# A fused linear-attention and MLP kernel: a division moved ahead of features, two transposes and a product regrouped, a new order table

## The chip, the cores and the metric

The kernel runs on one core of a Trainium2 chip. The core has five engines that run side by side: TensorE (PE, matrix products and transposes into PSUM), VectorE (DVE), ScalarE (ACT), GpSimd (POOL, used here to issue transfers and to make constants) and SyncE (SP, which issues transfers). The metric is the device time of one execution in microseconds (us); lower is better.

## The reference

Cosformer attention over 8 batches, 8 heads, 576 positions, 64 dimensions, then an MLP with a squared ReLU:

```python
q_p, k_p = phi(q, cos_w, sin_w), phi(k, cos_w, sin_w)   # relu(x)*cos(pos), relu(x)*sin(pos): 128 features
kv  = einsum('bhsf,bhsd->bhfd', k_p, v)
z   = sum(k_p, axis=2)
num = einsum('bhsf,bhfd->bhsd', q_p, kv)
den = einsum('bhsf,bhf->bhs', q_p, z)[..., None] + 1e-06
x   = (num / den), laid out as (4608, 512)
h   = x @ w_in                                           # (4608, 2048)
out = relu(h)**2 @ w_out                                 # (4608, 512)
```

## The kernel before

**Tiling.** A batch's 576 positions are four query blocks j = 0..3 of 128 and a tail of 64; the tails of all batches form a ninth token set, "batch 8". For each batch the attention part does: load k, q, v; features (`cos b.j`, `sin b.j`, each for k and q at once, on ACT or DVE; `.t` is the tail); `kv b` (40 small products into one PSUM tile, with z in a column of ones) and its copy `kvz b`; q's features transposed (`qT`, by TensorE and a copy `qTc` for batches 0 and 1, by a transposing DMA `qTd` on SP for later ones); `num b.j` (8 products); `div b.j` on DVE (den + eps, reciprocal, multiply) into x; x transposed (`xT`/`xTc`, or `xTd` by DMA). `vs b.i` spreads v into a tile that all batches share.

**The MLP.** Token blocks are 256 wide (tok 0 = queries 0 and 1, tok 1 = queries 2 and 3). Batch 0, batch 1 and half of batch 2 use plain products: `H b.s.tok half` is 8 matmuls of 128x256 for two blocks of hidden units, followed by a relu `r` (ACT or DVE) and, for pairs, a square `q`. `Y0.a0..15` and `Y0.b0..15` are batch 0's output products, one hidden block each. The other products use a scheme of seven half-size products in place of eight (Strassen's, in Winograd's form): `G b.s.P1..P7` for the first matrix and `Y b.P1..P7` for the second, with sums `xs`, `w1s`, `w2t`, `S` on DVE and copies between PSUM tiles (`seed`, `u2`, `s5`) and results (`c11`, `c12`, `c21`, `c22`) on ACT and DVE. Stores are `Y b.st0/1`.

**What sets the order.** Each engine runs its instructions in program order. The first part (`begin`, L1312) is written by hand: constants, loads, batch 0's k features, the features of queries 0 and 1, kv in two halves, their numerators and divisions. `warm` puts in matmuls on zeros so that TensorE is not idle; their results are not used. After that comes the table `ORDER`: a list of operation names in the order of emission, a `*` meaning ACT where ACT or DVE would do. `Plan.run` (L220) walks the table, picks tile slots with a small model of due times (`plan.given` tells it when things of the first part are ready) and `o.emit` then puts each operation out. The times in the model decide slots only; on the chip each operation waits for its data.

**PSUM.** Tiles of the MLP come from the pool `x` with 6 one-bank slots; `n` (numerators and kv) has one slot of two banks.

**Transfers.** POOL issues, in this order: k's tails of batch 0, q of queries 0 and 1, v, q of queries 2 and 3, w1 in four quarters (`w1.0`–`w1.3`; cast to bf16 on the way), q's tails, w2's first quarter, and then `loads_of_1` (L1433): q and its tails, k and its tails, w2's second quarter, v, w2's third and fourth quarter, all for batch 1 but for w2. After that come batch 2's loads as the table places them (`ldv2.0`, `ldq2`, `ldk2`, ...). The tile of q and k, `kq`, has one slot, so q1 waits until batch 0's features have read it. Half `vs` tiles of batch 1 lie in the slots of `y`; from batch 2 on they share one slot of their own. `Y0.x4` is the first product that reads w2's second quarter, `Y0.x8` the third, `Y0.x12` the fourth; `w2t1` needs all four. SP issues the later batches' loads, the transposing DMAs and most stores.

**The pair of output products.** `plan_pair` (L1122) has two shapes. With `apart` (batch 8 only, before) the first product's two token halves go into two one-bank tiles, each half of the second product is added and copied out alone at the very end, and the stores are cut into halves. Without it both halves share a tile. In both, `P1` is one operation of 16 matmuls, and one or two `seed` copies follow it.

Of the kernel before, what the change touches and what calls it, by code (L numbers as in the profile page):

```python
# [11 lines left out]
F32 = mybir.dt.float32  # L12
# [10 lines left out]
ORDER = """  # L23
qT0.2 xT0.k2 xT0.k3 qTc0.2 qT0.3 xTc0.k3* H0.0.00.0 xTc0.k2 qTc0.3* num0.2 H0.0.00.1 div0.2
H0.0.00.2 H0.1.00.0 H0.1.00.1 H0.1.00.2 H0.0.00r num0.3 H0.1.00r* xT0.2 H0.3.00.0 div0.3 xTc0.2*
H0.2.00.0 H0.3.00r xT0.3 H0.1.01.0 xTc0.3* H0.0.11.0 H0.1.10.0 H0.0.11r* H0.1.00q* H0.1.11.0
f0.t1 H0.1.10r H0.2.11.0 H0.1.11r* w1s1 f0.t0* H0.0.10.0 H0.2.00r* H0.1.01r* H0.2.11r H0.0.01.0
H0.0.10r* H0.1.11q* qT0.4 H0.1.10q Y0.a0 Y0.a1 H0.0.01r* Y0.b0 qTc0.4* Y0.a2 H0.3.11.0 Y0.a3
H0.3.11r Y0.b1 H0.3.00q Y0.b2 H0.3.11q* H0.2.10.0 w1s2 H0.3.01.0 H0.2.10r* sin1.3 H0.3.10.0
H0.3.01r* cos1.t Y0.b3 sin1.t H0.3.10r* H0.2.01.0 cos1.0 H0.3.10q* sin1.0 qT1.4 Y0.a4 H0.2.01r*  # L30
cos1.2 ldv2.0 Y0.b4 qTc1.4* sin1.1 Y0.b5 sin1.2* Y0.b6 cos1.3 Y0.a5 cos1.1* vs1.0 Y0.a6 Y0.a7
vs1.1 Y0.b7 ldq2 vs1.2* qT1.3 qT1.0 qTc1.3 ldk2 kv1 qTc1.0 ldkt2.0 H0.1.01q qT1.1 ldkt2.1 kvz1*
qT1.2 qTc1.1* ldv2.2 Y0.b8 Y0.b9 qTc1.2* num1.1 Y0.b10 div1.1 ldqt2.1 Y0.a8 H0.3.01q* Y0.a9
ldqt2.0 w1s4 Y0.a10 xT1.1 num1.2 Y0.b11 div1.2 Y0.b12 ldkt3.1 Y0.b13 ldkt3.0 w2t1 Y0.b14 vs2.0*
num1.0 ldqt3.0 xT1.2 Y0.a11 div1.0 xTc1.1* ldqt3.1 ldv2.1 Y0.b15 xTc1.2* Y0.a12 w2t2 Y0.c11*
Y0.a13 xT1.0 num1.3 xTc1.0* Y0.a14 div1.3 Y0.a15 Y0.c10* H1.1.01.0 Y0.c00* Y0.st1 w2t3 Y0.c01*
xT1.3 H1.2.00.0 xTc1.3* Y0.st0 H1.1.01r H1.2.01.0 sin2.0* sin2.1 H1.2.10.0 cos2.2 cos2.0*
H1.1.10.0 cos2.1 H1.2.10r sin2.3* H1.3.00.0 qTd2.0 cos2.3 H1.3.10.0 H1.3.00r* sin2.2 cos2.t*
H1.2.01r H1.0.01.0 vs2.1* H1.3.10r qTd2.1 H1.1.11.0 vs2.2 sin2.t* H1.2.00r H1.0.00.0 H1.0.01r*
w2t4 kv2 ldv3.2 H1.0.00r* H1.1.11r* H1.3.00q H1.0.10.0 H1.1.01q kvz2* ldv3.0 ldk3 num2.1  # L40
H1.0.10r* H1.1.00.0 div2.1 ldq3 H1.1.10r* H1.0.11.0 ldqt4.1 H1.1.00r* H1.3.10q H1.2.11.0
H1.1.10q H1.0.11r* H1.1.00q* H1.1.11q num2.2 H1.3.11.0 div2.2 H1.2.11r* H1.3.01.0 H1.3.11r*
ldkt4.1 vs3.2 H1.3.11q num2.3 ldv4.2 H1.3.01r* Y1.P1 div2.3 H1.3.01q* Y1.S1 xTd2.1 num2.0
Y1.seed vs3.0* Y1.S2 Y1.P2 div2.0 ldv3.1 Y1.P6 Y1.c11 xTd2.0 Y1.S3 num1.4 Y1.u2* sin3.1 Y1.P5
cos3.0* qTd2.2 sin3.0 cos3.1 sin3.3* Y1.P7 sin3.2 qTd3.0 Y1.s5* cos3.2 cos3.3* Y1.S4 H2.1.10.0
qTd3.1 vs3.1 H2.0.11.0 sin3.t* div1.4 H2.1.10r* H2.0.00.0 cos3.t* ldv4.0 H2.1.00.0 H2.0.00r ldk4
# [36 lines left out]
div5.4 cos7.0* G5.2.P6 G5.2.P2 sin7.0 Y4.P7 G5.1.c21q* xTd5.2 Y4.c12 vs7.1* G5.2.u2 Y4.st0
G5.3.P1 G5.2.c11r G5.2.P7 G5.3.seed cos7.1 G5.2.P3 sin7.t* G5.3.P5 Y4.c22 qTd7.0 G5.3.P2 cos7.3
G5.3.s5* G5.3.P6 G5.3.c11r* G5.2.c22r Y4.P4 G5.3.c11q* G5.1.c12q sin7.3 G5.3.u2* G5.2.P4 cos7.2
Y4.c21* G6.0.P1 cos7.t* G5.3.P7 qTd7.1 G5.3.P3 G5.2.c21r* G5.3.c22r kv7 G6.0.seed G5.2.c12r
G5.3.c22q* G5.3.c12r qTd7.2 G6.0.P2 G5.3.P4 G5.3.c12q G6.0.c11r* Y5.P1 G5.3.c21r* xs6.1 xs6.2
kvz7* Y5.S1 G5.3.c21q* G6.0.P5 num7.0 Y5.seed xs6.3 G6.0.P6 Y5.S2 G6.1.P1 G6.0.u2* Y5.P2
G6.0.s5* div7.0 G6.1.seed Y5.S3 num7.1 G6.1.P2 G6.1.P6 div7.1 G6.0.P3 G6.1.u2* G6.0.P7 Y5.S4
G6.1.c11r* xTd7.0 G6.1.P7 Y5.c11* num7.2 G6.1.P5 xs6.4 Y5.P5 Y4.st1 div7.2 G6.1.s5* G6.0.c22r  # L90
G6.1.c22r num7.3 Y5.s5* G6.1.P3 G6.1.c22q Y5.P6 G6.1.c11q* G6.1.c12r G6.2.P1 Y5.u2 G6.0.P4
div7.3 G6.1.P4 Y5.P7 G6.1.c21r* G6.0.c12r xTd7.1 G6.2.seed G6.1.c12q G6.0.c21r* G6.2.P5 Y5.c22
G6.1.c21q* G6.3.P1 G6.2.P6 G6.2.s5* Y5.P3 G6.2.u2* Y5.P4 Y5.c12 G6.3.seed G6.3.P6 Y5.c21*
G6.2.P2 G6.3.u2 Y5.st1 G6.3.P5 G6.2.c11r* G6.2.P3 G6.3.s5 G6.2.P7 G6.3.P2 G6.2.c22r G6.3.P3
G6.3.c11r* G6.3.P7 G6.3.c12r G6.3.c11q* G7.0.P1 G6.3.c22r num7.4 G7.0.seed G6.2.P4 G6.3.c22q
G6.3.P4 G6.2.c21r Y6.P1 G6.3.c21r* xs7.1 xs7.2 G6.2.c12r G7.0.P5 G6.3.c21q Y6.seed G7.1.P1 xs7.3
G7.0.P6 G6.3.c12q G7.0.P2 G7.0.s5 Y6.P2 G7.0.c11r* Y6.S1 G7.1.seed G7.0.P3 Y6.S2 Y6.c11* G7.1.P6
# [184 lines left out]
def kernel(  # L282
# [836 lines left out]

    def plan_pair(b, apart=False):  # L1122

# [424 lines left out]
```

## Time and profile before

| what | value |
|---|---|
| median of 3 runs | 274.11 us (273.96 to 275.32) |
| profiled execution, its time | 273.9 us |
| its span, first to last instruction | 271.8 us |
| TensorE busy | 263.3 us, 97% of the span |
| DVE, ACT, POOL busy | 226.7 (83%), 187.6 (69%), 28.9 (11%) |
| granted TensorE clock, mean | 0.998 |
| moved by DMA | 53.00 MB |

Times in the text are microseconds from the start of the span. A busy share is that of the whole span; the warming matmuls on zeros count as busy. A wait of TensorE is told with what released it. "To landing" is the time from a transfer's issue until its data is there. The "DMA share" of a stretch is the mean busy share of the 16 transfer engines, and can come out a little above 1 when packets overlap.

### The profile page before, as it was taken

The page shows a single profiled execution, that of the slowest core. Times are in us where ns is not written, and L with a number is a line of the kernel's source. Part 1 is how long each engine was busy: PE and PEld are TensorE (multiplying, and loading weights), DVE is VectorE, ACT ScalarE, POOL GpSimd, SP SyncE. Part 2 cuts the span into 40 slices and gives each one's busy share as a digit, 9 for nine tenths or more (in the row PEclk, how much of TensorE's full clock was granted, in tenths as well). Part 3 has the DMA queues.
Part 4 walks back from the last instruction along what each step waited for, and adds up shares of the span by engine and source line. Part 5 has one row for each costly group of instructions (what it writes and reads, how often), then busy time and mean ns, then how long its engine had stood idle before and what let it go on. Part 6 is the DMA issues. An engine that isn't in the chain of part 4 may idle for free.

```text
span 271.8 us, 6753 instructions
## 1 busy us (share of the span) xinstructions
PE 263.3 (97%) x2787; PEld 224.4 (83%) x2792; DVE 226.7 (83%) x403; ACT 187.6 (69%) x292; POOL 28.9 (11%) x47
## 2 busy tenths in 40 slices
PE   8799999999999999999999999999999999999994
PEld 3568767699778888989888998899888888888883
DVE  3874696998997999799989899989849978789952
ACT  5665695888567997889689968996554534955600
POOL 8924446200000000000000000000000000000000
PEclk9999999999999999999999999999999999999999
DMA  7999999897999999999997999680321021010215
GB/s 219 316 204 268 317 280 306 294 299 204 296 218 268 287 272 265 380 148 225 288 286 184 208 325 300 171 159 11 110 56 61 10 112 57 38 42 0 80 43 191
DMA packets 79006, 53.00 MB, mean 195 GB/s; under 512 B 52064, under 2 KB 74592, under 8 KB 78976
## 3 DMA queue, kind: packets, MB, share of 16 engines
q1 hardware_dynamic: 71344, 38.28, 55.0%
q0 software_dynamic: 7040, 13.76, 19.1%
q10 hardware_dynamic: 592, 0.52, 0.6%
q8 instruction: 22, 0.36, 0.5%
q14 instruction: 8, 0.07, 0.1%
HBM read 36.70 MB, written 9.44 MB: 170 GB/s over the span
## 4 chain that ended last, share of the span: by engine, by line
PE 84%; DMA 6%; DVE 4%; POOL 3%; issue 1%; ACT 0%; SPq 0%; POOLq 0%; ACTq 0%
PE ya L461 17%; PE yb L461 14%; PE hb L461 13%; PE hps L461 10%; PE hc L461 8%; PE ha L461 8%; PE yh L461 5%; DMA w1sb<-in_moe_w_in_dram 5%; PE kz L461 3%; PE num L461 3%; PE yc L461 1%; DVE gs L458 1%; DMA qpTt<-fet 1%; PE tq L622 1%; DVE fe L450 1%
## 5 line engine op out<-in xcount | busy, mean ns | idle before, releaser
L461 PEld LDWEIGHTS <-w1sb 128*128 128x128 bf16 x736 | 70.5, 98 | 10.8 <-issue 1.5
L461 PEld LDWEIGHTS <-gs 128*128 128x128 bf16 x512 | 49.7, 98 | 5.8
L461 PEld LDWEIGHTS <-gT 128*128 128x128 bf16 x448 | 43.1, 98 | 10.3 <-issue 0.5
L442 ACT ACTIVATE gT<-gT 128x1024 bf16<-128x1024 bf16 x38 | 39.6, 1060 | 4.0 <-DVE gT L455 2.0
L461 PE MATMUL hps<-xT,w1sb 128*128 128x256 bf16 x320 | 37.9, 273 | 1.2 <-ACT gT L436 0.8
L450 DVE TENSOR_SCALAR fe<-kq,cols 128x1024 bf16<-128x1024 f32 (+1 forms) x44 | 30.1, 722 | 5.2 <-DMA kq<-in_k_dram 3.5
L461 PEld LDWEIGHTS <-w1s 128*128 128x128 bf16 x312 | 29.8, 98 | 3.3
L461 PE MATMUL ya<-w2sb,gT 128*128 128x256 bf16 x256 | 30.6, 273 | 0.4 <-ACT yb L432 0.4
L461 PE MATMUL hb<-xs,w1sb 128*128 128x256 bf16 x208 | 30.1, 272 | 0.0
L448 ACT ACTIVATE fe<-kq,cols 128x1024 bf16<-128x1024 f32 (+1 forms) x28 | 27.6, 1027 | 2.9 <-DMA kq<-in_k_dram 1.6
L461 PE MATMUL ha<-xT,w1sb 128*128 128x256 bf16 x176 | 26.4, 273 | 0.0
L444 DVE TENSOR_TENSOR gT<-gT 128x1024 bf16<-128x1024 bf16 x34 | 23.0, 687 | 1.6 <-ACT gT L436 1.3
L604 DVE TENSOR_TENSOR xp<-num,den 128x512 bf16<-128x512 f32 (+1 forms) x33 | 22.2, 675 | 1.1
L455 DVE CUSTOM_DVE_ANT_0 gT<-hb,s 128x512 bf16<-128x512 f32 x26 | 17.8, 687 | 3.8 <-PE hb L461 3.7
L436 ACT ACTIVATE gT<-ha 128x512 bf16<-128x512 f32 x23 | 13.8, 600 | 9.5 <-PE ha L461 9.3
L436 ACT ACTIVATE gT<-hps 128x512 bf16<-128x512 f32 x27 | 15.6, 595 | 6.4 <-PE hps L461 6.4
L432 ACT COPY hb<-ha 128x512 f32<-128x512 f32 x26 | 15.2, 586 | 6.4 <-DVE gT L438 3.1
L458 DVE TENSOR_TENSOR gs<-gT 128x2048 bf16<-128x2048 bf16 x16 | 19.5, 1217 | 0.1
L455 DVE CUSTOM_DVE_ANT_0 gT<-hc,u 128x512 bf16<-128x512 f32 x26 | 17.5, 685 | 1.1 <-PE hc L461 0.9
L436 ACT ACTIVATE gT<-hb 128x512 bf16<-128x512 f32 x20 | 11.9, 601 | 6.7 <-PE hb L461 6.6
L461 PE MATMUL hc<-xs,w1s 128*128 128x256 bf16 x104 | 15.6, 272 | 0.0
L461 PE MATMUL hb<-xs,w1s 128*128 128x256 bf16 x104 | 15.6, 272 | 0.0
(111 smaller groups left out, 415.0 us busy)
## 6 DMA issues: line engine op xcount, KB each, us to landing
out_dram<-y SPq DMA_DIRECT2D x16, 512.0 KB, 3.6
vs<-in_v_dram SPq DMA_DIRECT2D x10, 512.0 KB, 4.6
kq<-in_k_dram SPq DMA_DIRECT2D x5, 1024.0 KB, 8.2
kq<-in_q_dram SPq DMA_DIRECT2D x5, 1024.0 KB, 9.9
w1sb<-in_moe_w_in_dram POOLq DMA_DIRECT2D x4, 512.0 KB, 12.0
w2sb<-in_moe_w_out_dram POOLq DMA_DIRECT2D x4, 512.0 KB, 10.7
kq<-in_q_dram POOLq DMA_DIRECT2D x2, 1024.0 KB, 11.5
kq<-in_k_dram POOLq DMA_DIRECT2D x2, 1024.0 KB, 11.7
```

Of the source, the lines that this page charges most:

```text
L432: (nc.scalar.copy if e == "ACT" else nc.vector.tensor_copy)(out=out, in_=in_)
L436: nc.scalar.activation(out=out, in_=in_, func=ACTF.Relu)
L442: nc.scalar.activation(out=out, in_=in_, func=ACTF.Square)
L444: nc.vector.tensor_tensor(out=out, in0=in_, in1=in_, op=ALU.mult)
L448: nc.scalar.activation(out=out, in_=in_, func=ACTF.Relu, scale=col)
L450: nc.vector.tensor_scalar(out=out, in0=in_, scalar1=0.0, scalar2=col, op0=ALU.max, op1=ALU.mult)
L455: nc.vector._custom_dve(dve_ops.TENSOR_ADD_SAT, out=out, in0=in0, in1=in1, s0=BIG, s1=0.0)
L458: nc.vector.tensor_tensor(out=out, in0=in0, in1=in1, op=op)
L461: nc.tensor.matmul(out=out, lhsT=lhsT, rhs=rhs, start=start, stop=stop, skip_group_check=True)
L604: nc.vector.tensor_tensor(out=x, in0=n4[:, :, :, 0:D].rearrange("p b (k l) d -> p b k l d", l=2), in1=r.rearrange("p b (k l) -> p b k l", l=2)
L622: nc.tensor.transpose(t[:, h, :], src, ident[:, :])
```

## The change

The table is new throughout. Its beginning, as it was:

```diff
-qT0.2 xT0.k2 xT0.k3 qTc0.2 qT0.3 xTc0.k3* H0.0.00.0 xTc0.k2 qTc0.3* num0.2 H0.0.00.1 div0.2
-H0.0.00.2 H0.1.00.0 H0.1.00.1 H0.1.00.2 H0.0.00r num0.3 H0.1.00r* xT0.2 H0.3.00.0 div0.3 xTc0.2*
-H0.2.00.0 H0.3.00r xT0.3 H0.1.01.0 xTc0.3* H0.0.11.0 H0.1.10.0 H0.0.11r* H0.1.00q* H0.1.11.0
-f0.t1 H0.1.10r H0.2.11.0 H0.1.11r* w1s1 f0.t0* H0.0.10.0 H0.2.00r* H0.1.01r* H0.2.11r H0.0.01.0
...
-cos1.2 ldv2.0 Y0.b4 qTc1.4* sin1.1 Y0.b5 sin1.2* Y0.b6 cos1.3 Y0.a5 cos1.1* vs1.0 Y0.a6 Y0.a7
```

and as it is:

```diff
+xT0.k0 sin0.2* cos0.3 xTc0.k0 xT0.k2 ldv2.0 cos0.2* qT0.2 sin0.3* qTc0.2 xT0.k3 xTc0.k2 qT0.3
+xTc0.k3* H0.1.00.0 num0.2 H0.1.00.1 H0.1.00.2 H0.0.00.0 H0.0.00.1 H0.0.00.2 div0.2 qTc0.3*
+num0.3 div0.3 xT0.2 H0.3.00.0 xT0.3 H0.2.00.0 xTc0.2 xTc0.3* H0.1.10.0 H0.1.10r H0.2.10.0
+H0.2.00r* H0.0.01.0 H0.0.01r* H0.1.01.0 H0.1.01r* H0.0.10.0 H0.2.10r* H0.1.11.0 f0.t1 H0.0.00r
+H0.1.00r H0.1.00q H0.3.00r Y0.a0 f0.t0* qT0.4 H0.0.10r H0.1.10q H0.0.11.0 H0.0.11r* w1s1 Y0.a1
+Y0.a2 H0.2.11.0 qTc0.4* H0.2.11r* w1s2 w1s4 Y0.a3 H0.2.01.0 cos1.3 H0.1.11r* H0.2.01r* H0.3.10.0
+H0.3.10r* H0.3.10q sin1.0* Y0.b0 Y0.b1 Y0.b2 Y0.b3 H0.3.01.0 H0.3.00q sin1.3* sin1.t cos1.t
+H0.3.11.0 H0.3.11r cos1.1 Y0.b4 H0.3.01r* Y0.b5 Y0.b6 Y0.a4 Y0.a5 cos1.2* sin1.1* qT1.4 qTc1.4*
+vs1.1* sin1.2 qT1.3 ldqt2.1 Y0.a6 Y0.a7 cos1.0 qT1.0 vs1.0 qTc1.3* vs1.2 kv1 H0.3.11q* qT1.1
+H0.1.01q Y0.a8 Y0.a9 Y0.b7 qTc1.1 kvz1* num1.1 ldq2 qTc1.0 qT1.2 H0.1.11q* Y0.b8 Y0.b9 Y0.b10
+div1.1 xT1.1 qTc1.2* num1.2 ldk2 H0.3.01q* ldkt2.1 w2t1 Y0.b11 Y0.b12 Y0.b13 Y0.b14 div1.2 xT1.2
+w2t2 xTc1.1* num1.0 ldqt2.0 div1.0 Y0.b15 xTc1.2* Y0.c10* w2t3 Y0.a10 vs2.0* Y0.a11 Y0.a12
...
+num2.3 H1.1.11q H1.3.11r* H1.3.01.0 H1.3.01r* H1.3.01q* Y1.P10 div2.3 num2.0 Y1.seed Y1.P11
+Y1.seed1 ldqt4.1 H1.3.11q vs3.2 Y1.P20 vs3.0* Y1.P21 Y1.c111* Y1.S1 Y1.S2 Y1.P6 xTd2.1 div2.0
+Y1.S3 Y1.c110 Y1.u2* cos3.0* sin3.1 cos3.1 cos3.2* sin3.0 sin3.2 sin3.3* num1.4 div1.4 cos3.3*
+Y1.P5 ldv4.2 Y1.S4 ldv3.1 vs3.1 H2.1.10.0 xTd2.0 xs2.1 H2.1.10r* qTd2.2 H2.0.11.0 H2.0.11r*
```

The rest of the code. In `plan_pair`, batch 1's pair is made with `apart` too (but with whole stores; `last` now marks batch 8's), and with `apart` the first product is two operations, P10 and P11, each with its own seed:

```diff
-    def plan_pair(b, apart=False):
+    def plan_pair(b, apart=False, last=False):
...
-        ys = [buf(p, [P, 2, DM], F32, "y") for p in (("vs", "y") if apart else ("y", "y"))]
+        ys = [buf(p, [P, 2, DM], F32, "y") for p in (("vs", "y") if last else ("y", "y"))]
...
-                        start = first and hb == 0 and (t == 0 or len(spaces) > 1)
+                        start = first and hb == 0 and (t == t0 or len(spaces) > 1)
...
-            after = [w[1]] + (seeds if apart else [e11])
+            after = [w[1]] + ([p1] if apart else [e11])
...
-        after = [w[0], sum5.get(b), begun.get(0)]
-        p1 = prod(1, A, block(0, 0), lambda: w2_block(0, 0), True, after, accs)
+        p1, seeds = None, []
+        for t in range(len(accs)):
+            t1 = t + 2 // len(accs)
+            after = [w[0], sum5.get(b), begun.get(0)] if p1 is None else [p1]
+            p1 = prod(1, A, block(0, 0), lambda: w2_block(0, 0), True, after, accs[t : t + 1], t, t1)
+            seeds.append(
+                ev(
+                    f"seed{t or ''}",
+                    {"ACT": act((t1 - t) * n)},
+                    lambda e, t=t, t1=t1: copy(e, run[:, t:t1, :], bank(accs[t])),
+                    [p1],
+                    [accs[t], run],
+                )
+            )
...
-            p = prod(2, A, lhs, lambda: w2_block(1, 0), False, seeds, accs[t : t + 1], t, t + 1)
+            after = seeds[t : t + 1]
+            p = prod(2, A, lhs, lambda: w2_block(1, 0), False, after, accs[t : t + 1], t, t + 1)
...
-                plan_pair(b - 1)
-        plan_pair(B, True)
+                plan_pair(b - 1, b == 2)
+        plan_pair(B, True, True)
```

In the part written by hand, one of qpT's copies goes from DVE to ACT; the features of queries 2 and 3, the turns (transposes) of x's first two blocks and their copy, and the call of `loads_of_1` go out of it, so that the division of the second head group follows the first directly:

```diff
-            copy("DVE", qpT[0, 0][:, j, 0:HH], tqs[j][0][:, :, :])
+            copy("ACT" if j else "DVE", qpT[0, 0][:, j, 0:HH], tqs[j][0][:, :, :])
...
         div_mul(na[:, :], dens[0][:, 1], x_of(0, 2))
-        cos_part("DVE", 0, 2, q_)
-        sin_part("ACT", 0, 2, q_)
         warm(2, "x0")
         nb = numerators(1)
         div_den(nb[:, :], dens[1])
-        tx = spare("x1", [P, 2, 2, P], BF16, "tx")
-        for kb in range(2):
-            turn_x(tx[:, kb], kb)
-        dst = xT[0, 0][:, 0:2, :].rearrange("p k (j c) -> p k j c", j=2)
-        copy("ACT", dst, tx[:, :, :, :])
         for i in range(2):
             part = nb[:, :, 2 * i * E1 : 2 * (i + 1) * E1]
             div_mul(part, dens[1][:, 1, :, 2 * i : 2 * (i + 1)], x_of(2 + i, 3 + i))
-        cos_part("DVE", 0, 3, q_)
-        sin_part("ACT", 0, 3, q_)
         warm(4, "x0")
-        loads_of_1()
```

They become table operations (`xT0.k0`, `xTc0.k0`, `cos0.2`, `sin0.2`, `cos0.3`, `sin0.3`), and `loads_of_1` is called in the table's loop when the last of the four features has been put out:

```diff
+    def plan_query(j, after):
+        made = []
+        for name, part in (("cos", cos_part), ("sin", sin_part)):
+            made.append(
+                plan.op(
+                    f"{name}0.{j}",
+                    both(0.62, 0.41),
+                    lambda e, part=part: part(e, 0, j, q_),
+                    [after],
+                    [fe[0, 1]],
+                )
+            )
+        return made
...
+        fq0 = {(1, j): plan_query(j, q0) for j in (2, 3)}
+        first = fq0[1, 2] + fq0[1, 3]
...
             o.emit(o.engine)
+            if o in first:
+                first.remove(o)
+                if not first:
+                    loads_of_1()
```

The due times given to the table's model are changed by some tenths too.

241 lines of the change are left out of this document (120 added, 121 removed).

## The prediction

> **What bounds the kernel now.** I read the page's head first, then TensorE's busy time in stages that I cut at its own landmarks, then its waits.
>
> ```profile
> span 271.8 us, 6753 instructions
> PE 263.3 (97%) x2787; PEld 224.4 (83%) x2792; DVE 226.7 (83%) x403; ACT 187.6 (69%) x292; POOL 28.9 (11%) x47
> ```
>
> ```profile
> 14.00:17.45 3.45, 3.17 (x38) 2.08 (x36) 2.52 (x8) 2.40 (x5) 0.06 (x1) 1.00 1.23 205
> 17.45:22.51 5.06, 4.76 (x59) 4.00 (x57) 3.56 (x9) 2.45 (x4) 2.08 (x3) 1.00 1.25 211
> 22.51:36.90 14.39, 14.34 (x119) 11.42 (x121) 8.73 (x13) 9.78 (x16) 8.20 (x11) 1.00 1.12 317
> 36.90:51.91 15.01, 14.85 (x164) 9.17 (x165) 12.39 (x24) 11.09 (x17) 6.23 (x9) 1.00 1.10 292
> ...
> 70.00:83.00 13.00, 11.69 (x122) 9.91 (x120) 12.67 (x21) 7.54 (x10) 0.00 (x0) 1.00 1.13 243
> 83.00:268.10 185.10, 185.04 (x1989) 165.57 (x1986) 160.81 (x277) 130.70 (x206) 0.00 (x0) 1.00 0.63 163
> ```
>
> Columns: stage, its length, then busy time of PE, its weight loads, DVE, ACT, POOL, then granted clock, DMA share, GB/s. From 22.51 us on, TensorE (PE) is the bound. It idles 0.05 in 22.51–36.90, 0.16 in 36.90–51.91, 1.31 in 70–83 and 0.06 in the 185 us after that. So the change, which keeps every product, can win at most about 1.6 us here, plus what the start gives. The DMA share is above 1 from 14 us to 52 us: the transfer engines have no free time there.
>
> ```profile
> PE hps L461 <- ACT gT L436: 0.8, 1, 0.8
> ...
> PE ya L461 <- ACT yb L432: 0.4, 1, 0.4
> PE hps L461 <- DMA w1sb<-in_moe_w_in_dram: 0.3, 1, 0.3
> ```
>
> These are the waits the change could touch: the wait for w1's third quarter (to 22.51), the one of Y1.P2 for its seed (to 70.61) and the one of a batch 2 product for a PSUM buffer (to 81.98). The last has a chain behind it: ACT evicts only after `sin3.t`, which waited 2.17 us for qTd2.2 to free its tile.
>
> Next, the transfers on POOL's queue: when each was issued (timeline), and how long until it landed (DMA issues, cut to one issue each).
>
> ```profile
> 17.39 0.90 POOL L502 DMA_DIRECT2D kq<-in_q_dram  x1 [4.13 <-ACT xT L432]
> 26.52 0.76 POOL L418 DMA_DIRECT2D w2sb<-in_moe_w_out_dram  x1
> 28.19 0.75 POOL L512 DMA_DIRECT2D vs<-in_v_dram  x1 [0.92 <-DMA w2sb<-in_moe_w_out_dram]
> 35.95 0.80 POOL L512 DMA_DIRECT2D vs<-in_v_dram  x1
> ```
>
> ```profile
> w2sb<-in_moe_w_out_dram POOLq DMA_DIRECT2D x1, 512.0 KB, 10.3
> ...
> vs<-in_v_dram POOLq DMA_DIRECT2D x1, 512.0 KB, 9.9
> ...
> w2sb<-in_moe_w_out_dram POOLq DMA_DIRECT2D x1, 512.0 KB, 11.1
> ```
>
> The same sum for each issue gives the landings, in queue order: w2's first quarter 27.9, q1 30.8, k1 33.9, w2's second quarter 26.52 + 10.3 = 36.8, v1's halves 28.19 + 9.9 = 38.1 and 39.4, w2's third 42.8, its fourth 35.07 + 11.1 = 46.2, v2's first half (35.95, 11.6) 47.55. They come one after another without a gap, so each costs those behind it its own time: a 512 KB half of v 1.3 us (36.8 to 38.1 to 39.4).
>
> ```profile
> 36.68 0.39 PE L622 MATMUL tq<-ident,fet 128*128 128x128 bf16 x4
> 36.90 3.62 PE L461 MATMUL yh<-w2sb,gT 128*128 128x512 bf16 x15
> ```
>
> The first product that reads w2's second quarter (Y0.a4) starts at 36.90, a tenth after it landed, and nothing before it waits. TensorE and the queue are level there.
>
> **The change, part by part.**
>
> *POOL's queue.* The new table has ldv2.0 (512 KB for batch 2) ahead of cos0.2 and sin0.3. But batch 1's loads are now issued inside the table loop, once the last of the four features of queries 2 and 3 has been issued. So ldv2.0 goes to POOL before q1, k1, w2's later quarters and v1, where it went last before. It waits for no data: the vs tile has no earlier user. Everything from q1 to w2's fourth quarter lands 1.3 us later: k1 35.2, w2's second quarter 38.1, v1's last piece 41.1, w2's third 44.1, its fourth 47.5. Behind that the queue is as long as before, so q2 and k2 are not later.
>
> Bounds for that price: 0 if the queue had room, 1.4 by v2's own turn (46.2 to 47.55). I take 1.3, because the share above 1 leaves no room. The Trainium skill ("DMA: Bandwidth & Descriptors", queues, rings and completion order) says that each engine consumes a ring's descriptors in ring order, and the trace agrees, as landings follow issues. The same page (anatomy of one DMA) puts the moving part at bytes/436e3 us, for 512 KB an estimate of 1.2 us; with it the term below would be 0.1 smaller.
>
> Now TensorE. Ahead of w2's second quarter the new table has 16 H products (0.873 each by the 8-matmul rows), eight Y0 steps (0.437), two numerators (0.24) and three transposes (0.22): 18.6 us. From 17.45 that ends at 36.05. I find four small waits on the way: the second division's buffer (0.15), div0.3 before xT0.3, which now has one product ahead of it and not two (0.3), Y0.a0 (0.55) because f0.t1 holds DVE until q0's tail lands (25.54 in the trace) and four DVE steps of 0.68 follow, and a PSUM buffer (0.1). So it is ready at 37.15 and goes on at 38.15. Before, the same point (without qT1.4, which moves behind it) was 36.68. **+1.47.**
>
> After it: kv1 needs the last DVE features and vs1.2. Nine DVE steps from k1 at 35.2 (four features of 0.73, two tails of 0.5, two squares of 0.69, one relu of 0.68) and two spreads (0.69, 0.6) end at 42.5; TensorE is there at 42.3. With a wait's usual lag **+0.25** (0 to 0.6). w2t1 needs all of w2, so DVE stands at it until 47.5 and div1.2 and div1.0 come 1.2 (w2t) + 1.1 each behind; xT1.2 and xT1.0 wait 0.2 and 0.1 by my count, and one more division could. **+0.4** (0 to 1.0).
>
> *The division ahead of the features, qpT's copy on ACT.* ACT sat idle 0.55 at 11.24–11.79, so the copy (0.59) is free there, and DVE's v spread and the second kv sums come 0.45 earlier. den1 starts at about 14.35 and not 15.26, xp is done at 15.5 and not 16.45. But q's second half lands at 7.12 + 7.7 = 14.8, three features on ACT at 0.67 each end at 16.9, and qT0.3 starts at 16.95 (16.99 before); w1's first quarter lands at 17.4 too. So the first H product stays at 17.45. x's turns move 0.22 of transposes and one 0.47 copy into the table, beside the features. **0** here, and w2's second quarter covers it: TensorE has 1.0 to spare before 38.15. Without that cover its cost is the +0.47 that 37.15 stands behind 36.68.
>
> *Y1's first product in halves.* Two half seeds (0.37 by the last `y<-ya` 128x256 copy) in place of one of 0.57, and the second product goes at once, with nothing between; the 0.36 seed wait goes. But P6 comes next and needs S2. From num2.1 DVE has three divisions (1.1), three squares (0.69), one relu, vs3.2 (0.6) and two sums (1.22): 9.1 us; TensorE has 8.5 to do until P6. P6 then waits 0.6 where before it came right after P2. **0** (−0.36 to +0.3). The two extra PSUM banks that Y1 now holds come back with c110 and c111 before batch 2's products.
>
> *The wait at 82 us.* In the new table H2.1.10's and H2.0.11's evictions stand ahead of sin3.t on ACT, so the 2.17 us that ACT stands there no longer hold a PSUM buffer. **−0.98** (the idle of 80–90 in 10 us steps; −1.3 to 0).
>
> After 83 us the same products run, dense before, and the tail of 3.7 us (c111 0.42, two stores) is the same steps. Sum: 1.47 + 0.25 + 0.4 + 0 − 0.98 = **+1.1**: span 272.9. The profiled run took 273.9 for 271.8, and the median is 274.11, 0.2 above it, so 274.11 + 1.1 = **275.2 us**.
>
> **The rivals.**
>
> *DVE keeps the delay (slower).* If the later w2 and k1 push DVE's whole list (12.67 of 13.00 busy in 70–83), the wait at 82 us stays: S4, xTd2.0 and qTd2.2 all hang on it. For it: in 60–83 the chain before already runs through DVE's xp, gT, gs and fe. Against: w1s4 (1.22) moves from 45.7 to about 32 us, which DVE has free. It decides from where DVE, not TensorE, starts S1. Price: 1.47 + 0.25 + 0.4 + 0 = 2.1 with no gain, 276.2; with the upper ends (0.6, 1.0) 3.1, 277.2.
>
> *The transfer is hidden.* If queue order does not pass the 1.3 on, w2's second quarter lands at 36.8 and TensorE's own 37.15 decides: +0.47, no late kv1 or w2t1, −0.98 later: −0.5, 273.6. With the small early waits absent as well (36.85, +0.17) and the seed's 0.36 won, −1.2, 272.9. Against it is the DMA share.
>
> *The change doesn't do what it says.* The start gives nothing, as worked out, since w1 and q land when they did; that is in the forecast already and in both rivals.
>
> **How the numbers follow.** Forecast 0.45 (its own range 274.4 to 276.0), DVE rival 0.33 (276.0 to 277.2), hidden transfer 0.22 (272.7 to 274.1). The range 273.3 to 276.9 leaves out about the lowest third of the hidden case and the top of the DVE case, near 2 in 10. A measurement of this kernel can tell about 0.5% (1.37 us) from no change: 272.74 to 275.48. Faster takes a quarter of the hidden case and a little of landing jitter: 0.07. Slower takes a third of the forecast (0.15) and nearly all of the DVE rival (0.31): 0.46. The rest, 0.47, is the same.
>
> **What would show it.** Right: POOL issues a vs half before q1; w2's second quarter lands at about 38.1; a TensorE wait for DMA w2sb near 37–38 us of 0.5 to 1.3; Y0 done at 54 (51.9 before); no ACT gT wait near 82. Wrong: Y0.b4 before 37.5, or a vs issue behind w2's last quarter; a TensorE wait over 0.6 between 70 and 83 speaks for the DVE rival. A span below 271.5 would say that the queue had room and that my account of its order is wrong.

## The result, and the profile after

The changed kernel took 276.0 us (median of 20 runs, 274.25 to 276.95) beside 273.69 us for the kernel before (20 runs, 272.67 to 276.13): a ratio of 1.0069, 95% interval 1.0046 to 1.0091. That is some 1.9 us, 1.3 to 2.5: a small slowdown, but clear of the noise. Measured again on another chip, it was 1.0055 (1.0023 to 1.0087). The forecast was 275.2 us, so +1.1.

The head of the page of the changed kernel:

```profile
span 273.5 us, 6782 instructions
PE 264.0 (97%) x2787; PEld 224.0 (82%) x2792; DVE 223.8 (82%) x399; ACT 191.0 (70%) x298; POOL 29.0 (11%) x47
```

Its TensorE in stages, cut at the same landmarks as before (first H product, first product on w2's second quarter, end of Y0, last product; 21.70, between the first two rows, is no such landmark in the new order). The columns are those of the earlier table.

```profile
16.66:21.70 5.04, 4.91 (x61) 3.93 (x59) 3.05 (x9) 1.72 (x3) 1.53 (x2) 1.00 1.24 204
21.70:37.68 15.98, 14.27 (x115) 10.99 (x115) 11.60 (x17) 8.77 (x15) 8.55 (x12) 1.00 1.11 321
37.68:52.90 15.22, 15.11 (x166) 9.55 (x168) 13.49 (x25) 12.38 (x16) 5.63 (x8) 1.00 0.99 265
70.00:83.00 13.00, 12.50 (x132) 10.56 (x131) 12.29 (x23) 9.64 (x14) 0.00 (x0) 1.00 1.21 218
...
268.80:273.50 4.70, 0.00 (x1) 0.00 (x0) 0.42 (x1) 0.00 (x0) 0.00 (x0) 0.79 0.53 160
```

In the stage that ends with w2's second quarter TensorE is now idle for 15.98 − 14.27 = 1.71 us; before it was 0.05. In 70–83 it is idle for 0.50 (1.31 before). What follows the last product is 4.70 long (3.70 before). The waits of TensorE:

```profile
PE yh L462 <- DVE fet L451: 1.1, 1, 1.1
PE yh L462 <- DVE gT L445: 0.5, 1, 0.5
PE hps L462 <- DMA xT<-xp: 0.4, 1, 0.4
PE hc L462 <- DVE gT L456: 0.3, 1, 0.3
```

(All line numbers are 1 higher than before.) The first is the wait that the prediction looked for at 38 us. The name "DVE fet" is misleading: the product there starts at 37.68, and what landed at 37.66 is w2's second quarter. The timeline of POOL's queue and the landing time of that quarter show this:

```profile
14.32 0.76 POOL L513 DMA_DIRECT2D vs<-in_v_dram  x1 [0.92 <-DMA kq<-in_q_dram]
17.20 0.89 POOL L503 DMA_DIRECT2D kq<-in_q_dram  x1 [2.12 <-DVE qpT L433]
...
27.46 0.76 POOL L419 DMA_DIRECT2D w2sb<-in_moe_w_out_dram  x1 [0.80 <-DMA w2sb<-in_moe_w_out_dram]
```

```profile
w2sb<-in_moe_w_out_dram POOLq DMA_DIRECT2D x1, 512.0 KB, 10.2
```

A half of v (batch 2's) is issued at 14.32, ahead of q1 at 17.20, and w2's second quarter lands at 27.46 + 10.2 = 37.66.

The end of the kernel also looks different. First the changed kernel's DVE, ACT and SP timelines, then the kernel before:

```profile
263.66 0.69 DVE L459 TENSOR_TENSOR y<-yb,ys 128x512 f32<-128x512 f32 x1 [2.63 <-issue]
264.26 0.68 DVE L459 TENSOR_TENSOR y<-yc,yu 128x512 f32<-128x512 f32 x1
...
267.35 0.59 ACT L433 COPY y<-yb 128x512 f32<-128x512 f32 x1 [6.61 <-DMA out_dram<-y]
...
264.38 1.37 SPq L1070 DMA_DIRECT2D out_dram<-y  x2
...
270.56 0.49 SPq L1070 DMA_DIRECT2D out_dram<-y  x1
```

```profile
261.20 0.69 DVE L458 TENSOR_TENSOR y<-yc,yu 128x512 f32<-128x512 f32 x1 [1.11 <-PE yc L461]
...
261.92 2.31 SPq L1069 DMA_DIRECT2D out_dram<-y  x2
...
267.10 1.97 SPq L1069 DMA_DIRECT2D out_dram<-y  x3
```

The new table puts batch 8's c22 (`y<-yb,ys`) ahead of c12 (`y<-yc,yu`) on DVE. c12's inputs were ready when ACT's copy `yu` ended at 260.73, but it now stands behind c22, which needs the product P7. So c12 runs at 264.26 and not at 261.20, and the first stores of batch 8 are issued at 264.38 and not at 261.92. They meet the later ones: the last store is issued at 270.56, where before it was 268.58. The wait in SP's list is a store's:

```profile
SPq L1070 <- DMA out_dram<-y: 1.3, 1, 1.3
```

No such line stands in the list of the kernel before.

### The profile page after: what moved, and what is told of

The parts are those of the page before. It is cut to its first block, busy times and chain, and to the rows that moved or that the text cites. A ratio compares the mean times of both kernels' runs of the same rounds, so it can differ in the third digit from the quotient of the medians.

```text
span 273.5 us, 6782 instructions
## 1 busy us (share of the span) xinstructions
PE 264.0 (97%) x2787; PEld 224.0 (82%) x2792; DVE 223.8 (82%) x399; ACT 191.0 (70%) x298; POOL 29.0 (11%) x47
## 4 chain that ended last, share of the span: by engine, by line
PE 75%; DMA 14%; POOL 4%; DVE 2%; ACT 1%; issue 1%; SPq 0%; DVEq 0%; POOLq 0%; ACTq 0%
PE ya L462 17%; PE yb L462 14%; PE hb L462 12%; PE hc L462 8%; PE ha L462 8%; DMA w1sb<-in_moe_w_in_dram 5%; PE hps L462 4%; PE yh L462 4%; DMA kq<-in_q_dram 3%; DMA kqt<-in_k_dram 3%; PE kz L462 3%; DMA xT<-xp 3%; PE num L462 3%; PE yc L462 2%; POOL kq L503 1%; POOL w1sb L412 1%
## 5 line engine op out<-in xcount | busy, mean ns | idle before, releaser
L443 ACT ACTIVATE gT<-gT 128x1024 bf16<-128x1024 bf16 x35 | 36.7, 1061 | 2.1 <-DVE gT L456 1.7
L449 ACT ACTIVATE fe<-kq,cols 128x1024 bf16<-128x1024 f32 (+1 forms) x34 | 33.7, 1032 | 3.5 <-DMA kq<-in_k_dram 2.9
L451 DVE TENSOR_SCALAR fe<-kq,cols 128x1024 bf16<-128x1024 f32 (+1 forms) x38 | 25.4, 705 | 6.7 <-DMA kq<-in_k_dram 5.6
L445 DVE TENSOR_TENSOR gT<-gT 128x1024 bf16<-128x1024 bf16 x37 | 24.9, 685 | 0.2
L605 DVE TENSOR_TENSOR xp<-num,den 128x512 bf16<-128x512 f32 (+1 forms) x33 | 22.2, 675 | 1.1
L437 ACT ACTIVATE gT<-hps 128x512 bf16<-128x512 f32 x29 | 16.3, 592 | 7.7 <-PE hps L462 7.0
L433 ACT COPY u<-hb 128x512 f32<-128x512 f32 x21 | 12.3, 586 | 6.5 <-PE hb L462 6.4
L462 PE MATMUL yh<-w2sb,gT 128*128 128x512 bf16 x60 | 14.9, 379 | 1.7 <-DVE fet L451 1.1
L437 ACT ACTIVATE gT<-hb 128x512 bf16<-128x512 f32 x23 | 13.5, 596 | 4.1 <-PE hb L462 3.2
```

The costliest lines, as they stand in the source:

```text
L433: (nc.scalar.copy if e == "ACT" else nc.vector.tensor_copy)(out=out, in_=in_)
L437: nc.scalar.activation(out=out, in_=in_, func=ACTF.Relu)
L443: nc.scalar.activation(out=out, in_=in_, func=ACTF.Square)
L445: nc.vector.tensor_tensor(out=out, in0=in_, in1=in_, op=ALU.mult)
L449: nc.scalar.activation(out=out, in_=in_, func=ACTF.Relu, scale=col)
L451: nc.vector.tensor_scalar(out=out, in0=in_, scalar1=0.0, scalar2=col, op0=ALU.max, op1=ALU.mult)
```

## The experiments

Each run below that was timed was interleaved with the kernel before on its own chip; ratios are to that. Each profile shows one execution; the expectations call it a "look".

**e1: v2's half back behind the features.** Its word in the table goes behind `sin0.3`, so POOL issues it after all of batch 1's loads, as before the change.

```diff
-xT0.k0 sin0.2* cos0.3 xTc0.k0 xT0.k2 ldv2.0 cos0.2* qT0.2 sin0.3* qTc0.2 xT0.k3 xTc0.k2 qT0.3
+xT0.k0 sin0.2* cos0.3 xTc0.k0 xT0.k2 cos0.2* qT0.2 sin0.3* ldv2.0 qTc0.2 xT0.k3 xTc0.k2 qT0.3
```

> The changed kernel with one word of the table moved: ldv2.0 stands behind sin0.3, so POOL issues it behind all of batch 1's loads and w2, as before the change. Queue theory (v2's first half costs those behind it its own 1.3 to 1.5 us): w2's second quarter lands 1.3 us sooner counted from w2's first quarter (9.0 us behind it instead of 10.5), the 1.1 us wait of TensorE ahead of Y0.b4 shrinks to 0.3 or less, Y0 ends 0.8 to 1.1 us sooner, and the time is 0.8 to 1.1 us below the changed kernel: ratio to before 1.003 to 1.004. Rival (the new order of the H products and DVE's f0.t1 hold TensorE, not the transfer): the wait stays near 1 us, ratio 1.007 as the changed kernel.

Measured: 0.9998 (0.9969 to 1.0026). The interval does not overlap the changed kernel's 1.0046 to 1.0091, so the one word costs time: about 0.7%, 1.9 us, give or take 1 us, where 0.8 to 1.1 us was expected. (The changed kernel's second measurement, 1.0023 to 1.0087, just overlaps it.) Y0 ends at 52.62, against 52.90 in the first profile of the changed kernel and 54.11 in the mean of its four. w2's second quarter landed at 37.22, and the wait there is gone from TensorE's list:

```profile
PE hps L462 <- DMA xT<-xp: 0.6, 1, 0.6
...
PE yh L462 <- DVE gT L445: 0.3, 1, 0.3
```

**e2: the kernel before, with v2's half first.** The same part alone, put into the old table.

```diff
-qT0.2 xT0.k2 xT0.k3 qTc0.2 qT0.3 xTc0.k3* H0.0.00.0 xTc0.k2 qTc0.3* num0.2 H0.0.00.1 div0.2
+ldv2.0 qT0.2 xT0.k2 xT0.k3 qTc0.2 qT0.3 xTc0.k3* H0.0.00.0 xTc0.k2 qTc0.3* num0.2 H0.0.00.1 div0.2
...
-cos1.2 ldv2.0 Y0.b4 qTc1.4* sin1.1 ...
+cos1.2 Y0.b4 qTc1.4* sin1.1 ...
...
-        loads_of_1()
...
+            if o.name == "ldv2.0":
+                loads_of_1()
```

> The kernel before with ldv2.0 as the first word of the table and the loads of batch 1 issued behind it; nothing else moves. Queue theory: w2's second quarter lands at about 38.1 instead of 36.8, TensorE waits 1.2 to 1.4 us for it ahead of Y0.a4, and kv1 up to 0.3 more; some of it may come back at the wait near 82 us, which is 1.3 us long: the time is 0.4 to 1.5 us above before, ratio 1.0015 to 1.0055. Rival (the queue has room): no new wait, ratio 1.000.

Measured: 1.0018 (0.9984 to 1.0052), so unclear by time. The profile shows the delay (w2's second quarter at 38.27, against 36.82) and where TensorE meets it; `tq` is the last transpose ahead of that product, `kz` is kv1:

```profile
PE tq L622 <- DVE fet L450: 1.1, 1, 1.1
PE kz L461 <- DVE vext L432: 0.7, 2, 0.5
PE yh L461 <- DMA w2sb<-in_moe_w_out_dram: 0.5, 1, 0.5
```

Y0 ends 1.4 later (53.31 against 51.91), but kv3 starts 0.2 later (84.36 against 84.16). Against the second profile of the kernel before (52.13 and 83.25, below) it is 1.2 and 1.1, so whether the delay is absorbed between hangs on which profile one compares with.

**e3: the changed kernel with the old end.** From batch 8's P7 on, the table has the words of the kernel before.

```diff
-... Y8.S3 Y8.P7 Y8.c22
-Y8.st111 Y8.st101 Y8.c12 Y8.st001 Y8.st011 Y7.P4 Y7.c21 Y7.st1 Y8.P4 Y8.c21* Y8.st110 Y8.st100
-Y8.P20 Y8.c110 Y8.st0010 Y8.st0000 Y8.P21 Y8.c111 Y8.st0110 Y8.st0100
+... Y8.S3 Y8.P7 Y8.c12 Y8.st011 Y8.st001 Y7.P4 Y8.c22 Y8.st101 Y8.P4 Y7.c21 Y8.st111 Y7.st1 Y8.P20
+Y8.c21 Y8.P21 Y8.c110* Y8.st100 Y8.st110 Y8.st0000 Y8.st0010 Y8.c111 Y8.st0100 Y8.st0110
```

> The changed kernel with the last 30 words of the table as before the change: Y8.c12 and its stores ahead of Y8.c22 and its stores, c21 on DVE, c110 on ACT. Theory of the tail: the span ends 4.7 us after TensorE's last matmul instead of 3.7, because DVE stands at c22 until P7 is done, the four upper stores start 2.5 us later, and the last store waits at 270.56 for the transfer eight back, which shares its semaphore lane and landed at 270.46. With the old order the tail is 3.7 us again and the time 0.9 to 1.1 us below the changed kernel: ratio 1.003 to 1.004. Rival (the tail is the stores' own spread from run to run): the tail stays between 4.2 and 4.8, ratio 1.006 to 1.007.

Measured: 1.0024 (0.9994 to 1.0054), against 1.0069 and 1.0055 with the new end. What follows the last product is 3.8 us again. The wait for w2 is still there:

```profile
PE yh L461 <- DMA w2sb<-in_moe_w_out_dram: 1.4, 1, 1.4
```

**e4: both, and e4 again.** v2's half late and the old end.

> The changed kernel with both: ldv2.0 behind batch 1's loads, and the old tail. If the two are separate causes their gains add to 1.8 to 2.1 us: ratio 0.999 to 1.001, level with the kernel before. If part of the early gain is given back at waits further on (70 to 85 us, 175 us), the ratio stays at 1.002 to 1.004.

> The changed kernel with v2's half behind the features (so behind batch 1's loads) and the end of the kernel before, once more. Theory A: 0 to 0.7 us below the kernel before, as its first measurement gave 0.5 (interval -1.2 to +0.1). Rival (that difference was noise, and nothing is left in the rest of the change): within 0.3 of it.

Measured: 0.9981 (0.9957 to 1.0005), and on another chip 0.9969 (0.9945 to 0.9994). Without these two parts the rest of the change costs nothing, and may win 0.5 to 0.8 us: 273.25 us in the second measurement, where the kernel before had 274.49. This version beats the changed kernel and, narrowly, the kernel before: one of its two intervals ends below 1. Its spans (271.8, 271.2) do not tell where the gain is, since two profiles of the kernel before gave 271.8 and 271.1.

**The changed kernel again.** Three more profiles of it, the first from a timed run of several executions.

> The changed kernel once more, unaltered, beside the next three. Theory A (v2's half ahead costs about 1.2 and the new end 0.5 to 1.2, the rest nothing): 1.2 to 2.5 us over the kernel before. Rival (the price at the start comes back at the wait near 82 us, so the end alone is left): 0.5 to 1.2 over it. In the trace both expect the last matmul to lie 4.3 to 4.8 us before the end of the span, with y's last store issued by SP about 0.1 us after the landing of a store eight transfers earlier.

> The changed kernel, a third look: when w2's second quarter lands and when kv3 starts. Cushion: kv3 at 84.1 to 84.6 if the quarter lands by 38.3, over 85 if it lands at 39 or later, as in the two looks so far (37.66 and 84.52; 39.08 and 86.34). Rival (kv3 is set by something else): no such tie.

> The changed kernel, a fourth look, with the same expectation as the third.

Measured: 1.0055 (1.0023 to 1.0087); spans 274.3, 274.0 and 274.3 us. The transfers are not the same in each execution: w2's second quarter landed at 37.66, 39.08, 38.29 and 38.76 in the four profiles. This is the one of them in which it lands last; TensorE's rows that begin after a wait (start, length, last column the wait and its end):

```profile
16.29 0.62 PE L623 MATMUL tq<-ident,fe 128*128 128x128 bf16 x8 [0.48 <-ACT fe L449]
21.17 1.05 PE L462 MATMUL hps<-xT,w1sb 128*128 128x256 bf16 x8 [0.88 <-DMA w1sb<-in_moe_w_in_dram]
29.41 0.39 PE L462 MATMUL yh<-w2sb,gT 128*128 128x512 bf16 x1 [0.87 <-DVE gT L445]
39.10 2.32 PE L462 MATMUL yh<-w2sb,gT 128*128 128x512 bf16 x10 [0.59 <-DMA w2sb<-in_moe_w_out_dram]
45.72 1.46 PE L462 MATMUL yh<-w2sb,gT 128*128 128x512 bf16 x5 [0.67 <-DMA w2sb<-in_moe_w_out_dram]
```

These are 3.5 us of waits, the last one for w2's third quarter, which landed at 45.66; and nothing waits near 82 us. In the third profile the wait for the second quarter was 1.62, in the fourth 1.28 (at 38.84), and another of 0.29 at 49.44 was for w2's last quarter (landed 49.31). kv3 started at 84.52, 86.34, 84.73 and 85.73: the tie to the landing is there, though the third profile lies 0.13 above the band expected for it.

**e5: batch 1's first output product whole.** As e4, with one P1, one seed, one P2 and one copy for Y1.

```diff
-                plan_pair(b - 1, b == 2)
+                plan_pair(b - 1)
...
-... H1.3.01q* Y1.P10 div2.3 num2.0 Y1.seed Y1.P11
-Y1.seed1 ldqt4.1 H1.3.11q vs3.2 Y1.P20 vs3.0* Y1.P21 Y1.c111* Y1.S1 Y1.S2 Y1.P6 xTd2.1 div2.0
-Y1.S3 Y1.c110 Y1.u2* ...
+... H1.3.01q* Y1.P1 div2.3 num2.0 Y1.seed
+ldqt4.1 H1.3.11q vs3.2 vs3.0* Y1.P2 Y1.S1 Y1.S2 Y1.P6 xTd2.1 div2.0
+Y1.S3 Y1.c11 Y1.u2* ...
```

> As e4_again, but batch 1's first output product is whole again (one seed, one eviction). If the halves gain nothing because the last sums are late in either case (my step): the same time as e4_again within 0.3 us, a TensorE wait of 0.2 to 0.4 for the seed between 70 and 74 us, and kv3 again at 84.1 to 84.6. If the halves are worth their seed wait: 0.36 us slower than e4_again, and kv3 as much later.

Measured: 0.9975 (0.9949 to 1.0002), 273.47 us beside 273.25 for e4 on the same chip: no difference that this can tell. First e5's waits between 64 and 86 us, then the only one of e4's second profile:

```profile
70.35 1.91 PE L461 MATMUL ya<-w2sb,gT 128*128 128x256 bf16 x16 [0.41 <-ACT yb L432]
74.70 1.91 PE L461 MATMUL ya<-w2t,gs 128*128 128x256 bf16 x16 [0.32 <-DVE y L432]
```

```profile
80.81 1.03 PE L461 MATMUL hps<-xT,w1sb 128*128 128x256 bf16 x8 [0.60 <-DMA xT<-xp]
```

The halves remove the seed wait (0.41) and a second one (0.32). The wait of 0.60 for x's transposing transfer is not simply their price, since e4's first profile, with the same halves, lists no wait in this stretch. From kv2 to kv3 the eight profiles with the new table and the halves take 22.1 to 22.2 us where x's transfer is in time (five of them) and 22.7 to 22.9 where TensorE waits for it (three); e5 takes 22.6. kv3 was at 83.22, below the band that I expected; w2's second quarter landed earlier in that profile (36.19), which accounts for a part.

**e6: the kernel before, with Y1's halves alone.** (Batch 8's first product, split by the same code, stands as `Y8.P10 Y8.P11` side by side.)

```diff
-... H1.3.01r* Y1.P1 div2.3 H1.3.01q* Y1.S1 xTd2.1 num2.0
-Y1.seed vs3.0* Y1.S2 Y1.P2 div2.0 ldv3.1 Y1.P6 Y1.c11 xTd2.0 Y1.S3 ...
+... H1.3.01r* Y1.P10 div2.3 H1.3.01q* Y1.S1 xTd2.1 num2.0
+Y1.seed Y1.P11 Y1.seed1 vs3.0* Y1.S2 Y1.P20 Y1.P21 div2.0 ldv3.1 Y1.P6 Y1.c111* Y1.c110 xTd2.0 Y1.S3 ...
```

> The kernel before with batch 1's first output product as two halves and nothing else. If the halves gain nothing by themselves: within 0.3 us of the kernel before, the seed wait of 0.36 near 70.6 us gone, and as much more waited for the last sums or at 82 us. If they are worth their seed wait: 0.36 below the kernel before. A third way: the wait near 82 us stays (0.8) because that one hangs on the order of the feature tail and not on Y1; then kv3 stays at about 84.2.

Measured: 0.9995 (0.9968 to 1.0021), kv3 at 84.12. Its waits in 64–86 us:

```profile
70.11 0.42 PE L461 MATMUL num<-kvz,qpT 128*128 128x65 bf16 x8 [0.75 <-DVE xp L604]
...
81.94 1.91 PE L461 MATMUL hps<-xT,w1sb 128*128 128x256 bf16 x16 [0.45 <-ACT gT L436]
```

The seed wait has gone, a wait for a division (0.75) has come at the same place, and the one near 82 us is smaller (0.45 for 0.83).

**e7: v2's half read twice.** As e3, with a second read of the same 512 KB into the same tile.

```diff
-            eng.dma_start(out=vs[b, i][:, :, :, :], in_=src)
+            for _ in range(2 if (b, i) == (2, 0) else 1):
+                eng.dma_start(out=vs[b, i][:, :, :, :], in_=src)
```

> As e3 (the changed kernel with the end of the kernel before), but v2's first half is read twice, one transfer behind the other, so 512 KB more stand ahead of batch 1's loads; nothing else changes. Cushion (the idle time near 82 us takes up a late w2, but only as much as is there): w2's second quarter lands at 39.2 to 39.6 against 38.1, TensorE waits 0.6 to 1.6 there and more before Y0's last products, no wait is left near 82 us, and kv3 starts at 85.2 to 86.4, where it stood at 84.1 to 84.5 in every kernel whose quarter landed by 38.3; the time is 1.0 to 2.0 above e3's, so 0.6 to 1.0% above the kernel before. Rival (the transfers behind 64 us set kv3 whatever came earlier): kv3 again at 84.1 to 84.5 and the time of e3 within 0.5 us. Second rival (the price of the early transfer is not its turn in the queue): the quarter lands by 38.5.

Measured: 1.0252 (1.0194 to 1.031), far outside what either theory said. The reason is in the experiment. POOL's timeline and TensorE's waits:

```profile
29.54 0.75 POOL L513 DMA_DIRECT2D vs<-in_v_dram  x1 [13.89 <-DMA vs<-in_v_dram]
```

```profile
43.48 4.42 PE L461 MATMUL yh<-w2sb,gT 128*128 128x512 bf16 x10 [6.68 <-DMA w2sb<-in_moe_w_out_dram]
89.86 1.03 PE L461 MATMUL hps<-xT,w1sb 128*128 128x256 bf16 x8 [0.68 <-DMA xT<-xp]
```

The second read writes the tile of the first, so POOL held it, and every load behind it, for 13.89 us until the first had landed. It doubles a wait and not a turn in the queue, so it says nothing of the price of a turn. It does speak against the rival that the later transfers set kv3 whatever came earlier: w2's quarter is 5.3 us later than in e3, and kv3 is 8.4 later (92.92 against 84.50). Of the 3.1 us between the two, 2.3 lie in the rest of Y0 (17.56 us against 15.29), and there the granted clock had fallen to half after the wait. This is a part of that stretch (columns as in the stages above, so the clock is the third number from the end):

```profile
45.00:47.00 2.00, 2.00 (x6) 0.73 (x5) 1.97 (x5) 0.57 (x1) 0.30 (x1) 0.50 1.18 200
```

The ten products from 43.48 take 4.42 us; ten such products took 2.32 in the first profile of the changed kernel. A wait of 0.68 for x's transfer is still there at 89.86, so that wait is not simply free time that a late w2 uses up.

**The kernel before, a second profile.**

> The kernel before, a second look: w2's second quarter at 36.2 to 37.4 (36.8 in the first), so 1.0 to 1.6 earlier than in the changed kernel, and kv3 at 83.9 to 84.5 (84.16 in the first), with 0.4 to 0.9 us of waiting near 82 us. If the quarter lands at 38 or later here, the queue jitters as much without the change.

Measured: span 271.1 us, w2's second quarter at 36.62, kv3 at 83.25, below the expected band. Near 82 us nothing waits in this profile; the only wait in 64–86 us is the seed's:

```profile
70.83 1.91 PE L461 MATMUL ya<-w2sb,gT 128*128 128x256 bf16 x16 [0.36 <-ACT yb L432]
```

All profiles together, in us; "w2" is the landing of w2's second quarter, "after" is what lies between the end of the last product and the end of the span:

| kernel | v2's half | end | w2 | kv3 | last product ends | span | after |
|---|---|---|---|---|---|---|---|
| before | late | old | 36.82 | 84.16 | 268.1 | 271.8 | 3.7 |
| before, 2nd | late | old | 36.62 | 83.25 | 267.2 | 271.1 | 3.9 |
| changed | early | new | 37.66 | 84.52 | 268.8 | 273.5 | 4.7 |
| changed, 2nd | early | new | 39.08 | 86.34 | 269.9 | 274.3 | 4.4 |
| changed, 3rd | early | new | 38.29 | 84.73 | 269.3 | 274.0 | 4.7 |
| changed, 4th | early | new | 38.76 | 85.73 | 270.0 | 274.3 | 4.3 |
| e1 | late | new | 37.22 | 84.45 | 268.1 | 272.3 | 4.2 |
| e2 | early | old | 38.27 | 84.36 | 268.3 | 272.0 | 3.7 |
| e3 | early | old | 38.10 | 84.50 | 268.1 | 271.9 | 3.8 |
| e4 | late | old | 37.39 | 84.07 | 267.9 | 271.8 | 3.9 |
| e4, 2nd | late | old | 36.61 | 83.86 | 267.5 | 271.2 | 3.7 |
| e5 | late | old | 36.19 | 83.22 | 266.7 | 270.4 | 3.7 |
| e6 | late | old | 37.16 | 84.12 | 268.1 | 271.8 | 3.7 |
| e7 | early, twice | old | 43.44 | 92.92 | 276.5 | 280.6 | 4.1 |

Without e7: with the half early (six profiles) w2's second quarter lands at 38.36 in the mean and kv3 starts at 85.03; with it late (seven) at 36.86 and 83.88. So the early half moves the landing by 1.50 and kv3 by 1.15. The landings of the two groups do not overlap (37.66 is the earliest of the one, 37.39 the latest of the other); kv3's do. The new end makes what follows the last product 4.5 (five profiles, 4.2 to 4.7) and the old one 3.8 (eight, 3.7 to 3.9).

## Why the prediction came out as it did

The sign and the cause of the greater part were right; the sum of +1.1 was too small against a measured 1.9 and 1.5 us, though inside the range. That 275.2 came within 0.8 of 276.0 is in part luck: the kernel before measured 273.69 beside it, 0.4 below the 274.11 that the forecast started from. By stages, the mean of four profiles of the changed kernel against two of the kernel before (so the sum, 2.6, is that of these profiles and above the 2.3 between the medians):

| stretch | predicted | profiles |
|---|---|---|
| to the first product on w2's second quarter | +1.47 | +1.67 (38.48 − 36.81) |
| from there to the end of Y0 | +0.25 + 0.4 | +0.42 (15.63 − 15.21) |
| end of Y0 to kv3 | −0.98 | −0.46 (31.22 − 31.68) |
| kv3 to the last product's end | 0 | +0.22 (184.16 − 183.94) |
| behind the last product | 0 | +0.73 (4.54 − 3.81) |

*v2's turn in POOL's queue (+1.47): right, and shown.* POOL issues the half before q1, the quarter lands 1.50 later (1.3 forecast), TensorE waits there 0.6 to 1.6, and moving the one word back took about 0.7% off (e1). Counted from the landing of w2's first quarter, which takes out a part of the scatter, the quarter is 1.57 later (10.65 against 9.08 behind it). The small waits forecast on the way were there in the first profile: 0.51 at Y0.a0 (forecast 0.55), and about 0.3 at xT0.3 (forecast 0.3), which starts at 20.48 where the eight products from 19.31 leave off at 20.18. The Trainium skill ("DMA: Bandwidth & Descriptors", under where 436 GB/s comes from) has a lower limit too, about 358 GB/s for a core's traffic with HBM, by which 512 KB would take an estimated 1.46 us. The measured 1.50 lies nearer to this than to the estimate of 1.2 in the prediction, but landings that scatter by 1.4 us in one kernel do not settle a difference of 0.3.

*kv1 (+0.25) and w2t1 with its divisions (+0.4): the sum about right, the places wrong.* kv1 lists no wait in any of the four profiles. w2t1 was misread, in the text on the kernel before as well: it is a difference of two blocks from the first half of w2's rows, so it needs the first two quarters and not all four. In the fourth profile DVE starts it at 47.60, before the fourth quarter lands at 49.31:

```profile
47.60 1.22 DVE L459 TENSOR_TENSOR w2t<-w2sb 128x2048 bf16<-128x2048 bf16 x1
```

What did cost time, in the second and fourth profiles, was Y0's own products waiting for w2's third and fourth quarters (0.67 and 0.29), which I had not listed; the second profile of the kernel before has one of 0.25 for the third quarter too. That the sum comes out near the forecast is luck.

*The division, the features and x's turns (0): not contradicted.* The first H product started at 16.66, 17.49, 16.84 and 17.63 in the changed kernel, 17.45 and 17.35 before. The start follows the landings of q's second half and of w1's first quarter, which vary by that much. No run took this part alone; e4 bounds it together with the halves and the other reorderings, at −0.2% and −0.3%.

*Y1's halves (0): not contradicted, and the step was right in kind.* e5 and e6 show no difference by time, but can tell only about 1 us (e5 against e4) and 0.7 us (e6). P6 does wait for S2, as forecast, in all eight profiles with the new table and the halves, though for 0.2 us and not 0.6. In the first, S2 (`gs<-gs,gT`) ends at 71.90 + 1.23 = 73.13, and P6 (`yb<-w2t,gs`) starts at 73.19:

```profile
71.90 1.23 DVE L459 TENSOR_TENSOR gs<-gs,gT 128x2048 bf16<-128x2048 bf16 x1
```

```profile
70.16 3.00 PE L462 MATMUL ya<-w2sb,gT 128*128 128x256 bf16 x24
73.19 1.92 PE L462 MATMUL yb<-w2t,gs 128*128 128x256 bf16 x16
```

The 24 products in the first of these rows would fill 2.62 us at 0.109 a product (0.873 for eight, as in the prediction), and P6 starts 3.03 behind the first of them. The other 0.2 us is P2's first half, which waits for its half seed (that ends at 71.19, and it starts at 71.25); I had it go at once. So the wait of the kernel before is mostly still there, in two pieces too short for the lists above. In e5, with the product whole, and in e6 P6 follows P2 without a gap.

*The wait at 82 us (−0.98): mis-sized.* I took it for a fixed 0.98. The second profile of the kernel before has none of it: from Y0's end to kv3 it needs 31.12 us, the changed kernel 31.04 to 31.62, and the first profile of the kernel before 32.25. So the profile that I read had one of the longer ones, and about half of the forecast gain was there to be had.

*The end (0): the step that failed.* "The tail of 3.7 us ... is the same steps" held for the steps and not for their order. In the new table c22 stands ahead of c12 on DVE, and the four stores behind the two go out from 264.38 on, and not from 261.92. Putting the old order back (e3) took the stretch from 4.5 to 3.8, and the ratio from 1.0069 and 1.0055 to 1.0024; between e1 and e4 it took 0.0017. By these, the new end costs 0.5 to 1.2 us. The intervals of single pairs overlap, but all the profiles agree. How the new order lengthens the end is shown in part: in three of the four profiles of the changed kernel and in e1, SP's last store is issued 0.1 us after a store that ACT issued some 5 us earlier has landed; in the fourth it is not held, and the end is 4.3 all the same. This was to be read from the table, whose end was in sight: the prediction went by which operations there are and not by which of them stands first on DVE.

*A wait in the middle (+0.2).* In three of the four profiles of the changed kernel TensorE waits near 176 us (`hb <- u`, `hc <- gT`), and the stretch from kv6 to kv7 is 27.85 to 28.16 us; in the fourth of them, and in e1, e3, e4 and e5, it is 27.24 or 27.25. e3 has the same table up to there and does not wait, so the order alone does not make it. In the three, the load of batch 7's q landed 10.2 to 10.5 us after its issue, in the others 8.3 to 8.8. The first features that read it start late, and with them what DVE and ACT do for TensorE behind them. In the first profile it lands at 169.2:

```profile
169.31 0.75 DVE L451 TENSOR_SCALAR fe<-kq,cols 128x1024 bf16<-128x1024 f32 x1 [0.52 <-issue]
```

Why that load is slower in these three is not known.

*The rivals.* The hidden transfer is out: the quarter's landing moved. The DVE rival put the slower case on a wait that stays at 82 us; it did not stay. What came on top of the forecast is the end (+0.73 by the profiles) and the gain near 82 us that was only half there (0.52 missing). The rival had the better number for the wrong reason.

What stays open: the size of the early half's price. By time it is 0.5 us in the old table (e2, not resolved), 1.2 to 1.5 between e3 and e4, and 1.9 between the changed kernel and e1. Each of these differences carries about 1 us either way by its intervals, so they need not differ at all; landings that vary by 1.4 us between executions and a later stage that absorbs a delay only sometimes would spread them as well. Nor did a run tell apart whether the half costs by its bytes or by its place in POOL's queue (see the last section); e7, which was to price a second turn, held the queue in place of that. The DMA share of 1.11 to 1.24 up to 37.68 us speaks for the bytes.

## What to carry to other kernels

Where TensorE and a queue are level, a transfer that waits for nothing and is wanted late is dear if it is issued early: look at what stands behind it, and move it back before anything else is tuned. After a new order is made by any means, compare the last few operations on each engine by hand: an evacuation that is ready must not stand behind one that is not, since its stores meet the last ones. And a wait read in one profile is a sample: take a second profile before counting on its removal.

## What the runs showed of the hardware that was not expected

POOL never had more than eight transfers on the way in any of the 14 profiles: its issues wait for the landing of the transfer eight places ahead. In the changed kernel v2's half, eight places behind q's second half, was held 0.92 us until that landed (14.05, issue 14.32), and w2's second quarter, now eight places behind w2's first, was held 0.80 us until that landed (27.22, issue 27.46). So an added transfer delays the issue of the later ones too. Whether the chip or the way the program is built sets the eight, no run shows. At the end of the changed kernel SP's last store was held 1.3 us in the same way, until a store issued by ACT at 265.16 had landed at 270.46.

Landings vary between executions of the same code: q's second half at 14.05 to 15.03 in the four profiles of the changed kernel, w2's second quarter at 37.66 to 39.08, and with it the time of kv3 by 1.8 us.

In e7's wait of 6.68 us the granted clock fell: it was 0.50 from 43.5 to 47 us, behind the wait, and 1.00 again from 49 us on. Behind the wait of 1.62 us at the same place in the third profile of the changed kernel it was 1.00 (38.3 to 42).
